# Weight loads in halves of 128 partitions, first loads in order of need, weight differences spread over tile 1

## The chip, the core and the metric

The kernel runs on one core of one Trainium2 chip. Times are microseconds (us) of that core. A time quoted for a kernel is the median of its runs, with the lowest and highest beside it. A profile shows one single execution. Its span is the time from the first to the last instruction, 1.7 us less than the time of the same execution (310.6 against 312.32 in the profile of the kernel before).

TensorE multiplies matrices, VectorE and ScalarE work on elements, GpSimd copies, casts and issues some transfers, and SyncE issues most transfers. In profile lines these are PE (PEld: its weight load), DVE, ACT, POOL and SP.

## The reference

Sliding-window attention (window 32), then a gelu feed-forward layer over all tokens:

```python
# q, k, v: (8, 8, 576, 64) fp32
scores = np.matmul(q, k.transpose(0, 1, 3, 2)) / np.sqrt(64)
mask = np.abs(pos[:, None] - pos[None, :]) <= 32
attn = softmax(np.where(mask, scores, -1e9))
x = np.matmul(attn, v).transpose(0, 2, 1, 3).reshape(4608, 512)
h = x @ w_in                    # w_in: (512, 2048)
out = gelu_tanh(h) @ w_out      # w_out: (2048, 512)
```

## The kernel before

The 4608 tokens go through the feed-forward layer in nine tiles of 512 (tile 0 to tile 8). A batch of attention (576 tokens) is done beside each tile. In a tile `ffn_in` multiplies by w_in and ScalarE takes the gelu; then `ffn_out` multiplies by w_out. Tile 0 uses 64 plain matmul positions; the other tiles use a Winograd form of seven products instead of eight (112 positions). That form needs four differences of w_out blocks, T1 to T4, computed once by VectorE.

What attention does between the matmuls is written in plans: at position i, do these acts. s is a score (matmuls and Exp), m a mask, v the weighing of V with its sum, x the final multiplication into xT. w and u cast a loaded w_out block, c is a weight difference, d pairs a chunk of V. g = -1 is the "tail", the group of the last queries of a batch; its Exp result is called `pet`.

```python
PLAN = {4: "s0@0 s1@1 v-1", 16: "m0 m1 x-1", 33: "s2@0 v0@1 v1", 36: "m2", 44: "x0", 50: "x1",
        62: "s3@0 s4@1 v2", ...}
PLAN_0 = {0: "s2@0 m0 m1 w1", 4: "s3@1", 12: "w2", 17: "c1", 18: "s-1@0 m2 m-1", 24: "m3",
          28: "v-1@1 x-1", 32: "d0 d1", 36: "d2 d3", 44: "v0@0 v1@1 x0 x1", 46: "w3",
          48: "v2@0 v3@1", 52: "u3", 54: "x2", 58: "x3", 60: "c2"}
PLAN_1 = PLAN | {0: "s-1@1 m-1", 4: "s0@0 v-1", 10: "s1@1"}
```

Loads: the first batch's q and k go over two queues, then V, then w_in in four blocks of two halves each. The third block (i == 2) is split by partitions, 120 and 8:

```python
    def load_w_in(i, w, c0=0, c1=4):
        for r in (slice(0, 120), slice(120, 128)) if i == 2 else (slice(0, 128),):
            nc.sync.dma_start(w[r, c0:c1, :], w_in_v[r, c0:c1, 512 * i:512 * i + 512])
        return w
    ...
    qk(0, nc.scalar)     # q on SyncE's queue, k on ScalarE's
    tails_0("k")
    qk(2, nc.scalar)
    qk(4, nc.scalar)
    qk(6)
    load_table(exp_set)
    vs()
    wi = []
    for i in range(4):
        wi.append(load_w_in(i, stage_w(), 0, 2))
        load_w_in(i, wi[i], 2, 4)
```

The prologue does batch 0's attention. `turn` transposes a pair of heads, `turned` does this with the next pair's casts, and `spin` is dummy matmuls that keep TensorE's clock up:

```python
    cast_early(0, 0, split)
    turn(0, 0)
    cast_tails(0, nc.vector, odd)
    cast_early(0, 1, split)
    trans_out(0, 0, pts[0], nc.scalar.copy)
    spin(1)
    trans_tails(0, psO.tile([128, 8, 128], FP16, name="pt", tag="O"), odd)
    spin(1)
    turned(1, 1, nc.scalar.copy)
    score(0, 0, 0)
    spin(1)
    turned(2, 0, nc.scalar.copy)
    score(0, 1, 1)
    ...
```

Casts, differences and weighing:

```python
    def cast_w(w, dst, on_dve=(0, 1), cs=range(4), on_act=()):
        for c in cs:
            (nc.scalar.copy if c in on_act else nc.vector.tensor_copy if c in on_dve else nc.gpsimd.tensor_copy)(
                dst[:, c, :], w[:, c, :])
    def combine(i, eng):                        # T1 .. T4
        dst, x, y = wino["todo"][i]
        eng.tensor_tensor(dst, x, y, op=ALU.subtract)
    ...
            for fc in range(begun, NF):
                ffn_in(t, fc)
                if t == 1 and fc in (8, 12):
                    combine(fc // 4 + 1, nc.vector)
    ...
                elif kind == "v":
                    bb, gg = group(g)
                    o, d = weigh(bb, gg, at)   # sums with ones, then times V
                    ods[g] = (o, invert(bb, gg, d))
```

## Time and profile before

| | before |
|---|---|
| median of the first 3 runs | 309.49 us (308.96 to 309.91) |
| the profiled execution | 312.32 us, span 310.6, mean granted clock 0.982 |
| TensorE enters the w_in matmuls of tile 0 | 21.55 us |
| tile 1 starts | 63.73 us |
| tile 2 starts | 100.89 us |

The second row became the main lesson: the profiled execution lies 2.83 us above the median. The page lines that carry the argument stand in the prediction. One line more, the shares of the chain that ended last, by engine:

```profile
PE 76%; DMA 12%; DVE 6%; SPq 3%; ACT 1%; issue 1%; DVEq 0%
```

The reader is to see that 12% of the span, some 37 us, is spent waiting for transfers. All of it lies in the first 48 us; from tile 2 on the tiles run with TensorE full.

### The profile page before, as it was taken

The page shows a single profiled execution, that of the slowest core. Times are in us where ns is not written, and L with a number is a line of the kernel's source. Part 1 is how long each engine was busy: PE and PEld are TensorE (multiplying, and loading weights), DVE is VectorE, ACT ScalarE, POOL GpSimd, SP SyncE. Part 2 cuts the span into 40 slices and gives each one's busy share as a digit, 9 for nine tenths or more (in the row PEclk, how much of TensorE's full clock was granted, in tenths as well). Part 3 has the DMA queues.
Part 4 walks back from the last instruction along what each step waited for, and adds up shares of the span by engine and source line. Part 5 has one row for each costly group of instructions (what it writes and reads, how often), then busy time and mean ns, then how long its engine had stood idle before and what let it go on. Part 6 is the DMA issues. An engine that isn't in the chain of part 4 may idle for free.

```text
span 310.6 us, 7121 instructions
## 1 busy us (share of the span) xinstructions
PE 291.3 (94%) x2896; PEld 183.4 (59%) x2896; DVE 199.1 (64%) x444; ACT 190.4 (61%) x296; POOL 92.3 (30%) x143
## 2 busy tenths in 40 slices
PE   6888887899699999999999999999999999999994
PEld 2543443444378458845874587468746864684583
DVE  3473478579676867686768577857785743632452
ACT  4595762666646577667766775787478757705600
POOL 4432548110640505150516053323350040006000
PEclk9799999999789999999999999999999999999999
DMA  7999999999796799998999799969896013004013
GB/s 218 249 321 291 315 333 244 229 256 210 166 212 90 141 149 237 149 149 141 243 155 186 95 241 170 177 142 215 110 135 149 2 39 98 3 0 136 2 34 101
DMA packets 116564, 50.73 MB, mean 163 GB/s; under 512 B 97925, under 2 KB 109957, under 8 KB 116532
## 3 DMA queue, kind: packets, MB, share of 16 engines
q1 hardware_dynamic: 87190, 37.73, 59.5%
q0 software_dynamic: 27776, 10.83, 24.4%
q10 hardware_dynamic: 1566, 1.74, 1.7%
q8 instruction: 22, 0.36, 0.5%
q14 instruction: 10, 0.08, 0.1%
HBM read 36.70 MB, written 9.44 MB: 149 GB/s over the span
## 4 chain that ended last, share of the span: by engine, by line
PE 76%; DMA 12%; DVE 6%; SPq 3%; ACT 1%; issue 1%; DVEq 0%
PE mm L594 32%; PE mm L496 18%; PE ph L496 15%; DMA wst<-in_moe_w_out_dram 4%; DMA wst<-in_moe_w_in_dram 4%; PE ps_s L388 3%; PE ps_d L411 2%; DVE s L539 2%; DMA qr<-in_q_dram 2%; PE ps_o L421 2%; DMA tr<-in_k_dram 2%; SPq L200 2%; SPq L143 2%; DVE t L529 1%; PE mm L568 1%; PE py L568 1%
## 5 line engine op out<-in xcount | busy, mean ns | idle before, releaser
L496 PEld LDWEIGHTS <-w_in 128*128 128x128 f16 x576 | 56.3, 98 | 68.3 <-issue 2.7
L496 PE MATMUL mm<-xT,w_in 128*128 128x512 f16 x320 | 78.2, 379 | 0.7 <-DVE yo L574 0.7
L504 ACT ACTIVATE gT<-mm 128x512 f16<-128x512 f32 x80 | 47.7, 597 | 43.4 <-PE mm L496 42.6
L496 PE MATMUL ph<-xT,w_in 128*128 128x512 f16 x256 | 64.5, 379 | 1.2 <-ACT gT L504 1.1
L558 POOL DMA_DIRECT2D out_dram<-y x55 | 33.1, 610 | 94.9 <-DVE y L623 85.8
L594 PEld LDWEIGHTS <-s 128*128 128x128 f16 x512 | 50.1, 99 | 6.4
L539 DVE TENSOR_TENSOR s<-gT 128x512 f16<-128x512 f16 x64 | 27.2, 426 | 35.0 <-ACT gT L504 35.0
L594 PE MATMUL mm<-t,s 128*128 128x256 f16 x376 | 45.6, 276 | 0.0
L504 ACT ACTIVATE gT<-ph 128x512 f16<-128x512 f32 x64 | 36.4, 600 | 12.5 <-PE ph L496 12.5
L400 ACT ACTIVATE pe<-ps_s 128x960 f16<-128x960 f32 (+1 forms) x32 | 30.6, 975 | 16.6 <-PE ps_s L388 16.4
L594 PEld LDWEIGHTS <-gT 128*128 128x128 f16 x384 | 36.3, 99 | 7.0
L594 PE MATMUL mm<-w_out,gT 128*128 128x256 f16 x256 | 34.3, 280 | 0.0
L447 ACT ACTIVATE lt<-lt 128x480 f32<-128x480 f32 (+3 forms) x40 | 23.5, 587 | 1.3
L92 ACT ACT_TABLE_LOAD x17 | 21.8, 1283 | 3.1 <-issue 2.4
L446 ACT ACTIVATE lt<-ps_d 128x480 f32<-128x480 f32 (+2 forms) x29 | 16.0, 552 | 10.5 <-PE ps_d L411 7.4
L406 DVE TENSOR_TENSOR pe<-pe,band 128x960 f16<-128x960 f16 x28 | 18.5, 680 | 1.7 <-ACT pe L400 1.7
L175 POOL DMA_DIRECT2D V<-in_v_dram x20 | 17.9, 909 | 1.2 <-issue 0.9
L421 PEld LDWEIGHTS <-V 128*64 128x64 f16 x520 | 14.7, 112 | 4.4 <-DVE V L190 0.8
L594 PE MATMUL mm<-t,gT 128*128 128x256 f16 x128 | 16.3, 273 | 0.0
L388 PE MATMUL ps_s<-QT,KT 64*64 64x128 f16 (+3 forms) x576 | 14.1, 221 | 0.7 <-DVE KT L312 0.7
L539 DVE TENSOR_TENSOR s<-s,gT 128x512 f16<-128x512 f16 x32 | 13.9, 434 | 1.1
L594 PE MATMUL mm<-w_out,s 128*128 128x256 f16 x120 | 14.4, 273 | 0.0
(103 smaller groups left out, 320.4 us busy)
## 6 DMA issues: line engine op xcount, KB each, us to landing
kr<-in_k_dram SPq DMA_DIRECT2D x29, 256.0 KB, 9.0
qr<-in_q_dram SPq DMA_DIRECT2D x6, 1024.0 KB
wst<-in_moe_w_in_dram SPq DMA_DIRECT2D x6, 512.0 KB, 9.0
wst<-in_moe_w_out_dram SPq DMA_DIRECT2D x3, 1024.0 KB
V<-in_v_dram POOLq DMA_DIRECT2D x20, 128.0 KB, 8.4
qr<-in_q_dram SPq DMA_DIRECT2D x8, 256.0 KB, 6.1
vr<-in_v_dram SPq DMA_DIRECT2D x8, 256.0 KB, 6.3
out_dram<-y POOLq DMA_DIRECT2D x6, 192.0 KB, 6.3
```

The source lines that it names most:

```text
L92: nc.scalar.add_instruction(mybir.InstLoadActFuncSet(name=nc.get_next_instruction_name(), act_func_set_id=which, ins=[], outs=[]))
L175: nc.gpsimd.dma_start(V[:, c, :, :], v[b, :, 128 * c:128 * c + 128, :].rearrange("h p d -> p h d"))
L388: nc.tensor.matmul(ps[64 * half:64 * half + 64, h, 4 * n * r:4 * n * r + 4 * n].rearrange("k (j p) -> k j p", j=4)[:, :, p0 - q0:p1 - q0], ...
L400: nc.scalar.activation(pe, ps[:, :, 0:w], AF.Exp, scale=SCALE)
L406: nc.vector.tensor_tensor(pe, pe, m.rearrange("k (o j) p -> k o j p", o=1).broadcast_to(list(pe.shape)), op=ALU.mult)
L421: nc.tensor.matmul(o[64 * h:64 * h + 64, cols].rearrange("d (j p) -> d j p", j=4)[:, :, p0 - q0:p1 - q0], Vs[b % 2][:, slot, 2 * pr + h, : ...
L447: nc.scalar.activation(lt[:, 0:n], lt[:, 0:n], AF.Exp, scale=-1.0)
L496: nc.tensor.matmul(ph, w_in16[:, dc, fc * 128:fc * 128 + 128], xT[:, dc, t * 512 % RING:t * 512 % RING + 512], start=(dc == 0), stop=(dc = ...
L504: nc.scalar.activation(gTs[t][:, fc, :], phs[fc], AF.Gelu_apprx_tanh)
L539: nc.vector.tensor_tensor(dst, x, y, op=op)
L558: eng.dma_start(out_v[b, j, q0 + p:q0 + p + e, cols], yo[m:m + e, cols])
L594: nc.tensor.matmul(pys["apart"][:, 0:256] if apart else py[:, blk, :], lhsT, wino[w][:, f, :], start=(new and i % (8 if one else 16) == 0) ...
```

## The change

The intent is to reach tile 2 sooner: load the third w_in block as fast as the others, score the first pair before the second is transposed, and keep weight differences away from the tail's mask. The core of the diff:

```diff
-PLAN_0 = {0: "s2@0 m0 m1 w1", 4: "s3@1", 12: "w2", 17: "c1", 18: "s-1@0 m2 m-1", 24: "m3",
-          28: "v-1@1 x-1", 32: "d0 d1", 36: "d2 d3", 44: "v0@0 v1@1 x0 x1", 46: "w3",
-          48: "v2@0 v3@1", 52: "u3", 54: "x2", 58: "x3", 60: "c2"}
-PLAN_1 = PLAN | {0: "s-1@1 m-1", 4: "s0@0 v-1", 10: "s1@1"}
+PLAN_0 = {0: "s2@0 m0 m1 w1", 4: "s3@1", 12: "w2", 18: "s-1@0 m-1 m2", 24: "m3", 30: "v-1@1 x-1",
+          32: "d0 d1", 36: "d2 d3", 44: "v0@0 v1@1 x0 x1", 46: "w3", 48: "v2@0 v3@1", 52: "u3", 54: "x2", 58: "x3",
+          60: "c1"}
+PLAN_1 = PLAN | {0: "s-1@1 m-1", 4: "s0@0", 10: "s1@1", 14: "v-1", 22: "c3", 56: "c4"}
...
 
-        def qk(h0, other=nc.sync):
-            for src, dst, queue in ((q, qr, nc.sync), (k, kr, other)):
+        def qk(h0, queues=(nc.sync, nc.sync)):
+            for src, dst, queue in zip((q, k), (qr, kr), queues):
                 queue.dma_start(
...
     def load_w_in(i, w, c0=0, c1=4):
-        for r in (slice(0, 120), slice(120, 128)) if i == 2 else (slice(0, 128),):
-            nc.sync.dma_start(w[r, c0:c1, :], w_in_v[r, c0:c1, 512 * i:512 * i + 512])
+        nc.sync.dma_start(w[:, c0:c1, :], w_in_v[:, c0:c1, 512 * i:512 * i + 512])
         return w
...
     qk, tails_0, vs = load_early(0)
-    qk(0, nc.scalar)
+    qk(0, (nc.sync, nc.scalar))
     tails_0("k")
-    qk(2, nc.scalar)
-    qk(4, nc.scalar)
+    qk(2, (nc.scalar, nc.sync))
+    qk(4)
     qk(6)
...
 
-    def turned(g, i, copy=nc.vector.tensor_copy):
-        turn(g, i)
-        if g < 3:
-            cast_early(0, g + 1, split)
-        trans_out(0, g, pts[g], copy)
-
     def pieces(tag, name):
...
     cast_tails(0, nc.vector, odd)
+    trans_out(0, 0, pts[0], nc.scalar.copy)
+    spin(2)
+    trans_tails(0, psO.tile([128, 8, 128], FP16, name="pt", tag="O"), odd)
     cast_early(0, 1, split)
-    trans_out(0, 0, pts[0], nc.scalar.copy)
     spin(1)
-    trans_tails(0, psO.tile([128, 8, 128], FP16, name="pt", tag="O"), odd)
+    score(0, 0, 0)
+    turn(1, 1)
+    cast_early(0, 2, split)
+    trans_out(0, 1, pts[1], nc.scalar.copy)
     spin(1)
-    turned(1, 1, nc.scalar.copy)
-    score(0, 0, 0)
-    spin(1)
-    turned(2, 0, nc.scalar.copy)
+    turn(2, 0)
+    cast_early(0, 3, split)
+    trans_out(0, 2, pts[2])
     score(0, 1, 1)
     cast_vt(0)
+    sums_of(0)
     spin(1)
-    sums_of(0)
     score(0, 2, 0)
+    turn(3, 1)
+    trans_out(0, 3, pts[3])
+    sums_of(1)
     spin(1)
-    turned(3, 1)
-    sums_of(1)
     score(0, 3, 1)
...
     os[0], os[1] = bank(0), bank(1)
-    s1 = psS.tile([128, 2, 512], FP32, name="ps_o", tag="S1")
-    os[2], os[3] = s1[:, 0, :], pieces("S0", "ps_o")
-    for g in range(2):
+    s0 = psS.tile([128, 2, 512], FP32, name="ps_o", tag="S0")
+    os[2], os[3] = s0[:, 0, :], pieces("S1", "ps_o")
+    for g in range(3):
         times(0, g, os[g], groups[(0, g)], (0, 1, 2, 4, 5))
-    spin(1)
+    spin(1, 512, s0[:, 1, :])
     sums_of(3)
-    for g in range(2, 4):
-        times(0, g, os[g], groups[(0, g)], (0, 1, 2, 4, 5))
-    spin(3, 512, s1[:, 1, :])
+    times(0, 3, os[3], groups[(0, 3)], (0, 1, 2, 4, 5))
+    spin(2, 512, s0[:, 1, :])
     cast_v(0, 3)
     for c in range(4):
-        cast_w(wi[0], w_in16[:, :, 0:512], (3,), (c,), (1,))
+        cast_w(wi[0], w_in16[:, :, 0:512], (3,), (c,))
     spin(3, 512, pieces("D", "spin"))
...
                 ffn_in(t, fc)
-                if t == 1 and fc in (8, 12):
-                    combine(fc // 4 + 1, nc.vector)
+                if t == 1 and fc == 8:
+                    combine(2, nc.vector)
                 if t == 1 and fc in (3, 4, 5, 6):
...
                     cs = (0, 1) if g == 3 else range(4)
-                    cast_w(wo[g], w_out16[:, 4 * g:4 * g + 4, :], cs=cs, on_act=(1,))
+                    cast_w(wo[g], w_out16[:, 4 * g:4 * g + 4, :], cs=cs, on_act=(1, 3))
                     if g == 2:
                 elif kind == "u":
-                    cast_w(wo[g], w_out16[:, 4 * g:4 * g + 4, :], on_dve=(2,), cs=(2, 3))
+                    cast_w(wo[g], w_out16[:, 4 * g:4 * g + 4, :], on_dve=(2,), cs=(2, 3), on_act=(3,))
                     cast_tails(1, nc.gpsimd)
```

The new plan puts T1 at the end of tile 0 ("c1" at 60), T2 in the w_in phase of tile 1, and T3 and T4 at positions 22 and 56 of tile 1.

> **What bounds the kernel now.** I read the busy shares first, then the chain of waits, then the timeline where that chain is not TensorE.
>
> ```profile
> PE 291.3 (94%) x2896; PEld 183.4 (59%) x2896; DVE 199.1 (64%) x444; ACT 190.4 (61%) x296; POOL 92.3 (30%) x143
> ...
> PEclk9799999999789999999999999999999999999999
> DMA  7999999999796799998999799969896013004013
> ```
>
> TensorE is busy 94% of 310.6 us, so over most of the run only fewer matmuls would help, and the diff removes none. But PEclk has a dip in slices 11 and 12 (78 to 93 us), and DMA is full for the first 47 us. From 101 us on, the tiles run with TensorE busy 30.50 of 30.50 us (the windows view of 101 to 131.5): what is won before 101 us reaches the end unchanged. The chain of waits, early part:
>
> ```profile
> 17.10 11.50 DMA wst<-in_moe_w_in_dram
> 28.62 5.74 DMA qr<-in_q_dram
> 34.35 12.90 DMA wst<-in_moe_w_out_dram
> ...
> 47.61 1.63 DVE t L529
> 49.24 0.98 DVE pe L406
> 50.23 0.76 DVE pet L406
> ```
>
> From 17 to 47 us loads set the pace; then the weight difference T1 (L529) and two masks stand on the path. The windows view compares stretches of equal kind (columns: length, busy time of five engines, granted clock, DMA share, GB/s):
>
> ```profile
> 21.00:27.30 6.30, 5.11 (x24) 2.14 (x23) 3.92 (x9) 4.25 (x7) 1.49 (x2) 1.00 1.06 227
> 28.00:34.00 6.00, 6.00 (x29) 2.74 (x28) 2.12 (x9) 4.18 (x7) 3.53 (x6) 1.00 1.07 352
> 38.00:44.00 6.00, 4.36 (x91) 2.73 (x91) 5.95 (x12) 4.25 (x5) 2.18 (x4) 1.00 1.05 382
> ...
> 78.00:82.20 4.20, 1.10 (x37) 0.77 (x29) 4.11 (x7) 3.51 (x4) 2.52 (x3) 0.88 0.70 102
> 81.20:88.00 6.80, 5.80 (x47) 3.95 (x47) 3.37 (x8) 2.33 (x4) 5.27 (x8) 0.50 0.86 230
> ```
>
> Two things stand out. In 21 to 27.3 us the DMA is busy but moves 227 GB/s, against 382 for the same 2048-byte rows of w_out. That is when the third w_in block passes, the one loaded as 120 and 8 partitions: by its packets, one takes 140 to 190 ns there and 84 to 88 ns before and after. And in tile 1 TensorE works 1.10 of 4.20 us, then 6.8 us at half clock. The timeline there:
>
> ```profile
> 78.17 1.62 DVE L529 TENSOR_TENSOR t<-w_out,t 128x2048 f16<-128x2048 f16 x1
> 81.59 0.55 DVE L406 TENSOR_TENSOR pet<-pet,band 128x768 f16<-128x768 f16 x1
> 82.20 0.53 PE L411 MATMUL ps_d<-pet,ones 128*64 128x384 f16 x2 [3.10 <-DVE pet L406]
> 51.02 0.30 PE L411 MATMUL ps_od<-pet,ones 128*64 128x256 f16 x2 [1.77 <-DVE pet L406]
> ```
>
> Twice the tail group's mask (pet) comes late because VectorE computes a weight difference first; TensorE stands 3.10 us in tile 1 and 1.77 us in tile 0.
>
> **What the Trainium skill says.** DMA: Bandwidth & Descriptors, section "Why a DMA increments its semaphore by 16 and not by 1": a DMA is split over the largest number of engines up to 16 that divides its outer dimension, so 120 partitions take 15 engines and 8 take 8. The trace agrees: the 120-partition DMA shows one of its 16 completion marks at 16.84 us, straight after issue, and 15 from 22.78 us on. Its section "The descriptor swizzle" says that in a 128-partition load each engine writes one SBUF port; a 15-engine split need not, which would explain the doubled packet time; no run yet shows the cause. TensorE: Matmul & The Clock Gate, Part 1: about 3.4 us of idleness drops the clock to half, in free-running windows. The trace agrees: the idle stretch 79.0 to 82.2 us, then clock 0.50 for 6.83 us (two periods of 3.41). DMA page, "Issuing engines are not separate DMA queues": which engine issues a load changes no bandwidth; so the new queue assignment of the first loads can only reorder.
>
> **The change, part by part.**
>
> 1. *Halves of 128 partitions.* The slow stretch moved some 1.43 MB (227 GB/s by 6.3 us); at the 385 GB/s seen on either side this takes 3.7 us, a gain of 2.6 us. By engine: a normal engine needs 16 packets x 84 ns = 1.34 us per half block; the slowest engine landed the second block at 24.32, the third at 28.60, the fourth at 31.09 us. From 21.50 us (first half of the second block) five halves at 1.34 us end at 28.2 us, so 2.9 to 3.2 us earlier. Also two fewer DMAs share the eight completion lanes that SyncE rotates through. Everything queued behind shifts by about 3 us: q and k of batch 1, w_out, and later k of batch 2, whose last chunk landed at 68.72 us and released the VectorE casts at 68.80 us.
>
> 2. *First loads in order of need, first pair scored earlier.* The k tails landed at 7.00 us behind two k pairs on the other queue; I estimate 6.4. Score 0 no longer waits for the second pair's transposes (10.29 us): KL copied by about 7.8 us, so its Exp starts near 8.7 instead of 11.41. But ScalarE is busy 9.20 of 10.20 us between 10.4 and 20.6, and V chunk 3 (15.80 us) and w_in's first halves (18.52 and 19.83 us) land no earlier. My pass through the queues (Exp 1.0, Ln+Exp 1.22, QT copy 0.6, spread 0.65 us each) puts the last spread at 21.35 instead of 23.06 us; TensorE enters w_in about 2 us earlier. This is then overtaken by part 1 and is not added.
>
> 3. *Tile 0.* T1 leaves position 17 (1.63 us), m-1 goes ahead of m2 (about 1 us), the third chunk of each w_out block moves from GpSimd to ScalarE. The w_out 2 block lands at 47.25 - 3.2 = 44.0; ScalarE then casts two chunks (1.25), does the pet Exp (0.6), VectorE masks (0.75): v-1 runs at 46.6 instead of 51.02, a gain of 4.4, of which 1.2 is beyond the DMA shift. Position 44 follows at 50.5 (12 + 2 matmuls x 0.216, plus v-1 itself), where V chunk 3 of batch 1 (52.36 - 3.2, cast, pairing) is also just ready; was 54.94. Tile 1 starts at about 59.3 instead of 63.73.
>
> 4. *Tile 1.* VectorE's chain starts with the k casts at 65.5 (DMA shift only). From 68.80 to 82.14 it took 13.3 us, including both differences; one (1.62) leaves, and the wait for the last gelu is gone: pet is masked at about 77.0. v-1 now stands at position 14, behind 14 matmuls and score 1, so TensorE idles about 1.1 us for pet's Exp (score 1 needs its bank) instead of 3.1, and the half clock should not come. Position 16 is reached at 77.9 instead of 86.17.
> Not all of this stays. After pet, VectorE pairs V of batch 2, whose last GpSimd cast (ended 82.62) moves only to 78.3; then it owes M1 copy 0.65, masks 1.2, x-1 0.55, T3 1.22, U2 0.69, m2 0.65, pairing 0.84 twice, x0 0.7, C11 0.67, x1 0.7: that is 87.0, and v2 at position 62 waits for x1. So position 62 runs at 87.7 instead of 94.68: **7.0 us** gained. T4 (1.22) fits before position 80.
>
> Sum: part 1 gives 3.2, the pet waits and half clock a further 3.8 after VectorE takes some back. 309.49 - 7.0 = 302.5; I give 0.4 back for lags such as contended differences (1.62 instead of 1.22). **302.9 us.**
>
> **The rivals.**
> - *VectorE becomes the bound in tile 1.* T3 and T4 now fall where TensorE works (VectorE busy 9.11 of 13.00 us between 88 and 101); if they collide with evictions more than reckoned, 1.5 us more is lost: 304.5. For it: the list above is already VectorE end to end.
> - *The slow stretch is not the partition split* but HBM or the column block. Then part 1 is nothing, tile 0 gains 1 to 2, tile 1 about 3.5: 304.5 to 305.5. Against it: blocks 1, 2 and 4 read the same layout at full speed.
> - *Loads stay on the path through one lagging engine.* An instruction fetch of 16 KB takes 1.2 to 1.3 us of one engine (16, 28, 45, 61 us) and the last of 16 marks counts. Then the shift is 2 instead of 3 us: about 304.
> - *The half clock trips anyway*: 3.4 us back, 306.
> - *The early loads alone matter not at all*, since later loads bound the end: already assumed.
>
> **Range and chances.** The rivals cost 1 to 3.4 us each and rarely come together; gains beyond the sum would need the V casts of batch 2 to come earlier too, up to 2 us. Eight in ten: 300.6 to 305.8. The 2% line is 303.3, just above the estimate: faster 0.56, same 0.43, slower 0.01.
>
> **What would show it.** Right: 2048-byte packets near 84 ns and over 350 GB/s through the third block; its last landing near 25, w_out 2's near 44 us; T1 absent before v-1 in tile 0; tile 1 starting at 59 to 60; no half clock near 80 us; the w_in phase of tile 2 starting near 94 us instead of 101. Wrong: GB/s still near 230 in 21 to 25 us; VectorE waiting for k of batch 2 beyond 67 us; TensorE waiting on x1 or U2 for over 1.5 us in tile 1; clock 0.50 again.

## The result, and the profile after

| | before | after |
|---|---|---|
| median, same chip | 309.68 us (308.96 to 309.91, 4 runs) | 304.91 us (304.43 to 305.74, 4 runs) |
| ratio of fast runs | 1 | 0.9853 (0.9825 to 0.9880) |
| the profiled execution | 312.32 us, clock 0.982 | 304.9 us, clock 0.992 |

A ratio is the mean time of one kernel's fast runs over the mean of the other's fast runs of the same rounds, so not quite the ratio of the medians quoted. The kernel after is about 1.5% faster: inside the predicted range, but on the slower side, and not past the 2% that I had held likeliest. The gain is 4.8 us of medians, where I had reckoned 6.6.

The page of the kernel after, busy shares, granted clock by slices and the chain by engine:

```profile
PE 288.1 (95%) x2896; PEld 181.6 (60%) x2896; DVE 197.1 (65%) x445; ACT 190.6 (63%) x297; POOL 89.0 (29%) x141
...
PEclk9799999999999999999999999999999999999999
...
PE 83%; DVE 6%; DMA 4%; ACT 3%; issue 1%; SPq 1%; POOL 0%
```

The reader is to see three things against the lines of before. TensorE is busy 3.2 us less in all (291.3 to 288.1) with the same 2896 matmuls. The dip to 7 and 8 in slices 11 and 12 of PEclk is gone. And transfers carry 4% of the chain instead of 12%.

The timeline of the kernel after, at the places of the prediction (start, duration, engine, line, operation, output and inputs, and in brackets the idle time before it and what ended it):

```profile
25.99 1.89 PE L495 MATMUL ph<-xT,w_in 128*128 128x512 f16 x8 [1.13 <-ACT gT L503]
...
46.02 0.74 DVE L405 TENSOR_TENSOR pet<-pet,band 128x512 f16<-128x512 f16 x1 [1.24 <-ACT pet L399]
47.68 0.30 PE L410 MATMUL ps_od<-pet,ones 128*64 128x256 f16 x2
60.14 1.21 DVE L528 TENSOR_TENSOR t<-w_out 128x2048 f16<-128x2048 f16 x1
...
77.26 0.56 DVE L405 TENSOR_TENSOR pet<-pet,band 128x768 f16<-128x768 f16 x1 [0.27 <-ACT pet L399]
77.28 0.40 PE L387 MATMUL ps_s<-QT,KT 64*64 64x96 f16 x16 [0.88 <-ACT pet L399]
...
86.92 0.42 PE L420 MATMUL ps_o<-pe,V 128*64 128x96 f16 x14 [0.49 <-DVE xT L455]
```

In tile 0 the mask now waits for the Exp on ScalarE (1.24 us of VectorE idle), not for T1, and v-1 at 47.68 follows with no wait shown on TensorE. T1 runs at 60.14, at the end of tile 0. In tile 1 TensorE's largest wait is 0.88 us, for pet's Exp, where it was 3.10 us for pet's mask in the first profile of before. v2 waits 0.49 us for x1, as the prediction had said it would.

The chain of waits of the kernel after, in tile 1 (start, duration, what):

```profile
71.16 6.30 DMA qr<-in_v_dram
77.51 0.80 POOL V L283
78.33 0.42 DVE V L182
...
81.57 0.72 DVE t L528
```

Here is what now sets the middle of tile 1: V of batch 2 lands at 77.46 us, is cast on GpSimd and paired on VectorE, and VectorE's list from there (M1, the masks, T3 and x1) releases v2 at 86.92 us. In the kernel before, no transfer stood on the chain after 47.25 us.

The same places in the windows view (length, busy time of PE, PEld, DVE, ACT and POOL, granted clock, DMA share, GB/s):

```profile
21.00:25.30 4.30, 3.86 (x18) 1.67 (x17) 2.74 (x7) 2.44 (x5) 1.48 (x2) 1.00 1.05 390
...
74.00:78.20 4.20, 3.33 (x67) 2.04 (x66) 2.38 (x5) 3.90 (x6) 1.70 (x3) 1.00 0.99 118
78.20:83.00 4.80, 4.80 (x86) 3.94 (x86) 4.66 (x8) 3.38 (x6) 3.68 (x6) 1.00 1.03 283
```

The third w_in block passes at 390 GB/s instead of 227, and tile 1 runs at clock 1.00 where it ran at 0.50.

| milestone, us in the profile | before | predicted | after |
|---|---|---|---|
| third w_in block landed | 28.60 | near 25 | 25.29 |
| w_out 2 landed | 47.25 | 44.0 | 44.34 |
| TensorE enters w_in | 21.55 | 2 earlier | 20.38 |
| v-1 of tile 0 | 51.02 | 46.6 | 47.68 |
| tile 1 starts | 63.73 | 59.3 | 60.27 |
| pet masked in tile 1 | 81.59 | 77.0 | 77.26 |
| position 62 of tile 1 (v2) | 94.68 | 87.7 | 86.92 |
| tile 2 starts | 100.89 | near 94 | 93.48 |

By these two profiles the prediction was right: 7.4 us gained by tile 2, where it had said 7.0. By the clock on the wall the gain was 4.8. From the start of tile 2 both profiles take 209.7 us to their end (310.6 - 100.89 and 303.2 - 93.48), so nothing was given back later. Something was in the profile of before that is not in most of its executions.

### The profile page after: what moved, and what is told of

The parts are those of the page before. It is cut to its first block, busy times and chain, and to the rows that moved or that the text cites. A ratio compares the mean times of both kernels' runs of the same rounds, so it can differ in the third digit from the quotient of the medians.

```text
span 303.2 us, 7115 instructions
## 1 busy us (share of the span) xinstructions
PE 288.1 (95%) x2896; PEld 181.6 (60%) x2896; DVE 197.1 (65%) x445; ACT 190.6 (63%) x297; POOL 89.0 (29%) x141
## 4 chain that ended last, share of the span: by engine, by line
PE 83%; DVE 6%; DMA 4%; ACT 3%; issue 1%; SPq 1%; POOL 0%
PE mm L593 30%; PE mm L495 21%; PE ph L495 17%; PE ps_s L387 3%; PE ps_d L410 2%; DMA qr<-in_v_dram 2%; PE ps_o L420 2%; PE mm L567 2%; DMA tr<-in_k_dram 2%; PE py L567 1%; ACT gT L503 1%; DVE xT L455 1%; ACT lt L445 1%; PE ps_od L410 1%; SPq L347 1%
## 5 line engine op out<-in xcount | busy, mean ns | idle before, releaser
L495 PE MATMUL ph<-xT,w_in 128*128 128x512 f16 x256 | 64.5, 379 | 1.2 <-ACT gT L503 1.1
L593 PE MATMUL mm<-t,s 128*128 128x256 f16 x376 | 44.7, 273 | 0.0
L593 PE MATMUL mm<-w_out,gT 128*128 128x256 f16 x256 | 33.2, 273 | 0.0
L446 ACT ACTIVATE lt<-lt 128x480 f32<-128x480 f32 (+3 forms) x40 | 23.5, 587 | 1.3
```

Of the source, the lines that this page charges most:

```text
L446: nc.scalar.activation(lt[:, 0:n], lt[:, 0:n], AF.Exp, scale=-1.0)
L495: nc.tensor.matmul(ph, w_in16[:, dc, fc * 128:fc * 128 + 128], xT[:, dc, t * 512 % RING:t * 512 % RING + 512], start=(dc == 0), stop=(dc = ...
L593: nc.tensor.matmul(pys["apart"][:, 0:256] if apart else py[:, blk, :], lhsT, wino[w][:, f, :], start=(new and i % (8 if one else 16) == 0) ...
```

## The experiments

Three questions stood at first. Is it the split of partitions that slows the packets of all transfers in flight, and is it worth most of the gain? Is the half clock in tile 1 worth about 3 us in every run, or does it come in only some executions? And is the early scoring hidden behind the loads, or does it matter, through the clock or through the order? Where a text on record uses a letter, P is the theory of partitions and ports, and C that of the clock. Twelve runs were made, in three groups, each group on its own chip with its own runs of before (medians 310.37, 309.58 and 310.48 us). Ratios are to those, of fast runs alone. Half clock means that the records show a granted clock of 0.50.

### The kernel before once more, and with its idle stretch filled

The first is the kernel before, unchanged. The second does twelve dummy matmuls while TensorE waits for pet in tile 1:

```diff
                     bb, gg = group(g)
+                    if t == 1 and g < 0:
+                        spin(12, 512, pieces("D", "spin"))
                     o, d = weigh(bb, gg, at)
```

> The kernel before, unchanged. Theory A (the half clock in tile 1 belongs to some executions only): most executions show a mean granted clock of 0.99 or more and a span near 307.8 us; those with 0.98 are 2.5 to 3 us longer, like the profiled one (310.6 us, clock 0.982). Theory B (the timed executions all have the half clock and the profiled one was slow for another reason): clock 0.98 in all, spans spread without regard to the clock.

> The kernel before with 12 dummy matmuls (2.6 us) in the hole of TensorE in tile 1, ahead of the sums of the tail group. The hole itself stays, only the clock cannot drop. Theory A: no half clock near 81 us in the profile, span near 307.5 us, and the median of the timed runs moves less than 1 us, since most of them had no drop. Theory B: the median falls by about 3 us, to 306.5.

Measured: the unchanged kernel 311.83 us (309.21 to 314.84, 6 runs, the highest in the slow state), ratio 1.0026 (0.9972 to 1.0081); the filled one 310.42 us (309.81 to 311.59), ratio 1.0003 (0.9962 to 1.0045). The filled kernel, timeline and windows:

```profile
79.67 2.76 PE L231 MATMUL spin<-KT 128*128 128x512 f16 x12
82.48 0.35 PE L411 MATMUL ps_d<-pet,ones 128*64 128x384 f16 x2
```

```profile
77.50:82.00 4.50, 4.50 (x52) 2.19 (x51) 4.32 (x7) 3.97 (x5) 2.58 (x3) 1.00 0.96 128
82.00:88.00 6.00, 5.94 (x106) 4.47 (x105) 3.82 (x8) 3.05 (x6) 4.94 (x7) 1.00 1.14 268
```

The dummies fill the hole and the clock stays at 1.00 through 82 to 88 us, where before had 0.50. Tile 2 starts at 98.52 instead of 100.89. Yet the time does not move: 1.0003. The profile of the unchanged kernel says why. It has the hole and no half clock in tile 1. Tile 1 as a whole, first of the first profile of before, then of this second one (timeline line, then windows line):

```profile
63.73:100.89 37.16, 34.06 (x351) 21.89 (x351) 27.83 (x60) 23.74 (x35) 10.46 (x15) 0.91 1.08 193
```

```profile
84.16 0.35 PE L411 MATMUL ps_d<-pet,ones 128*64 128x384 f16 x2 [2.23 <-DVE pet L406]
```

```profile
66.56:100.19 33.63, 31.40 (x350) 20.52 (x350) 27.68 (x60) 23.74 (x35) 9.94 (x15) 1.00 1.14 198
```

The same program takes 37.16 us for tile 1 in one execution and 33.63 in the other. The second is 31.40 us of work and one wait of 2.23. So the half clock in tile 1 is not worth its 3 us in every run. Neither theory of the first expectation came as stated. Theory A wanted clocks of 0.99 or more in most executions; of the 17 of this group two have that, and they took 311.78 and 313.45 us. Ten lie at 0.986 to 0.988. A mean clock tells how many periods of half clock an execution had, but not where: the profiles with 0.985 to 0.987 show two of them (beside the end of the run), at 8 us (before again), at 10 and 44 us (filled), or at 9 and 81 us (the split of 112 and 16 below), the first profile with 0.982 three. So more than half of the executions of before (21 of the 39 in all groups have 0.984 to 0.988) seem to have two periods, and in only some of them one of the two lies in tile 1.

Why one and not the other? The records of the clock change only at multiples of 3.41 us, and so I took TensorE's busy share in each such stretch (a window), for 14 profiles. Of the windows at full clock, the last 10 us of the runs left out, every one with a share of 0.51 or less was followed by a window at half clock; none with 0.62 or more was; those between went either way. (In the last 10 us one with 0.50 was not followed by half clock. A window that is itself at half clock can be followed by another with more: 0.70 at 81.18 us in the first profile.) In the first profile of before, the hole fell into one window (77.76 to 81.18 us, share 0.39). In the second it lay across two (0.60 and 0.75). So it fits that a hole of 2 to 3 us is caught or not by where the windows happen to lie.

### The w_in halves alone, and the change without them

The first is the kernel before with only the load changed; the second is the kernel after with only the load put back:

```diff
-        for r in (slice(0, 120), slice(120, 128)) if i == 2 else (slice(0, 128),):
-            nc.sync.dma_start(w[r, c0:c1, :], w_in_v[r, c0:c1, 512 * i:512 * i + 512])
+        nc.sync.dma_start(w[:, c0:c1, :], w_in_v[:, c0:c1, 512 * i:512 * i + 512])
```

> The kernel before with the third block of w_in in halves of 128 partitions, nothing else. Theory (a 120-partition load slows every packet that is in flight with it): packets of the third block take 84 to 90 ns, the block's last landing comes near 25.5 us instead of 28.6, the last chunk of w_out block 2 near 44.3 instead of 47.25, and about 3 us of it reach the end: 306.5 us. Rival (the column block or HBM is slow there): still about 227 GB/s and 140 to 190 ns per packet between 21 and 27 us, time unchanged at 309.5. Second rival (loads are hidden once the masks wait for T1): the loads land 3 us earlier but the time falls by less than 1 us.

> The changed kernel with the third block of w_in again as 120 and 8 partitions. If the partition split carries most of the gain: 308 to 309 us, with packets of 140 to 190 ns back between 21 and 27 us. If the new plans carry it: 306 us or less.

Measured: alone 309.06 us (306.75 to 310.41), ratio 0.9940 (0.9892 to 0.9987); the change without it 308.34 us (307.43 to 313.88, the highest in the slow state), ratio 0.9920 (0.9872 to 0.9968). The windows view, first of the halves alone, then of the kernel after with 120 and 8:

```profile
21.00:27.00 6.00, 5.04 (x23) 2.11 (x22) 4.22 (x10) 4.11 (x7) 2.40 (x4) 1.00 1.05 385
```

```profile
21.00:27.00 6.00, 3.96 (x18) 1.48 (x16) 1.70 (x6) 2.66 (x5) 1.74 (x2) 1.00 1.07 230
```

The split decides the rate, with all else equal: 385 against 230 GB/s, and by the trace's transfer records (medians of each microsecond from 21 to 26 us) 84 to 88 ns against 139 to 181 ns a packet of 2048 bytes. The third block landed at 25.34 us in the first. That the split is the cause is shown. Its worth is smaller than the shift: 0.6%, some 1.9 us, although the loads come 3 us earlier; the 306.5 us that the theory expected were missed. In tile 1 TensorE still waits for pet's mask; the waits view (what waits, for what, total us, number, longest):

```profile
PE ps_d L410 <- DVE pet L405: 2.6, 1, 2.6
```

### Another split: 112 and 16

By the rule quoted in the prediction, 120 partitions go to 15 engines and 8 to 8; 112 and 16 both divide by 16. If a missing engine were the cause, this would be fast.

```diff
-        for r in (slice(0, 120), slice(120, 128)) if i == 2 else (slice(0, 128),):
+        for r in (slice(0, 112), slice(112, 128)) if i == 2 else (slice(0, 128),):
```

> The kernel before with the third block of w_in split as 112 and 16 partitions. Both parts divide by 16, so by the skill's page all 16 engines take part in each. Theory P (not the missing engine but the spread of an engine's rows over SBUF ports slows the packets): the packets are slow again, 130 ns or more and under 260 GB/s between 21 and 27 us. Theory E (the load that leaves out an engine is at fault): 84 to 95 ns and over 350 GB/s, block landed near 25.5 us.

One look: 309.32 us. The windows view:

```profile
21.00:25.00 4.00, 3.94 (x20) 1.67 (x18) 3.14 (x7) 2.11 (x3) 1.49 (x2) 1.00 1.07 241
```

It is as slow, 241 GB/s, 132 to 152 ns a packet (medians as above, 21 to 25 us), and the third block landed at 27.19 us. So by that rule it isn't the number of engines. What is left is which partitions each engine writes (by the same rule a 112-partition load gives each engine 7 partitions, not 8), or that a second, small load runs beside the large one: both slow splits have it, and no run separates the two. That several engines then write through one port would explain it; the trace has no record of ports, so this stays argued. By the way, this profile has one window of half clock in tile 1 (80.73 to 84.14 us, after a window of share 0.35), where the first profile of before had two.

### The plans alone, and the change with the old plans

The first puts only the plans, the places of T1 to T4 and the `on_act` of the casts into the kernel before; the second puts the old ones back into the kernel after:

```diff
-PLAN_1 = PLAN | {0: "s-1@1 m-1", 4: "s0@0 v-1", 10: "s1@1"}
+PLAN_1 = PLAN | {0: "s-1@1 m-1", 4: "s0@0", 10: "s1@1", 14: "v-1", 22: "c3", 56: "c4"}
   (and PLAN_0, combine and on_act as in the change)
```

> The kernel before with the new plans alone: weight differences T1 to T4 at their new places, m-1 ahead of m2, v-1 of tile 1 at position 14, a third w_out chunk per block on ScalarE. Theory (the masks come before the differences, but w_out block 2 still lands near 47.3 us and k of batch 2 near 68.7 us): v-1 of tile 0 near 50 us instead of 51, TensorE's wait for pet in tile 1 gone (under 1.2 us in all), no half clock near 81 us; 308 to 309 us, ratio 0.993 to 0.998. Rival (VectorE takes it all back with T3 and T4 among the evictions): ratio 1.00.

> The changed kernel with the old plans put back: halves of 128 and the new prologue alone. The halves alone gave 0.994. Theory (the two parts need each other: earlier loads are worth less while T1 and T4 sit ahead of the masks): ratio 0.990 to 0.994, with a wait for pet of over 2 us in tile 1. Rival (the parts simply add): ratio 0.988 or less.

Measured: alone 308.79 us (307.41 to 309.58), ratio 0.9975 (0.9927 to 1.0022); the change with the old plans 307.50 us (306.31 to 308.85), ratio 0.9939 (0.9889 to 0.9989). The timeline of the latter, then of the plans alone:

```profile
48.78 0.30 PE L410 MATMUL ps_od<-pet,ones 128*64 128x256 f16 x2 [1.56 <-DVE pet L405]
...
78.24 0.56 DVE L405 TENSOR_TENSOR pet<-pet,band 128x768 f16<-128x768 f16 x1 [0.25 <-ACT pet L399]
78.85 0.35 PE L410 MATMUL ps_d<-pet,ones 128*64 128x384 f16 x2 [2.23 <-DVE pet L405]
```

```profile
81.52 0.40 PE L388 MATMUL ps_s<-QT,KT 64*64 64x96 f16 x16 [0.88 <-ACT pet L400]
```

With the old plans both waits for pet are back, 1.56 and 2.23 us; with the new plans and the old loads 0.88 us for pet's Exp is left. So it is shown that the plans remove these waits.

What in them does it is not the same in both tiles. In tile 0 it is the order on VectorE, T1's place among it: the first profile of before has T1, then a mask, then pet's mask (the chain in the prediction). In tile 1 it is hardly the place of T4. In the line at 78.24 above, with the old plans, VectorE itself stood idle for 0.25 us until ScalarE had finished pet's Exp (78.21 us), and T4 was over at 75.83. In six of the seven profiles with the old plans pet's mask begins within 0.1 us of the end of pet's Exp; only in the first profile of before did it begin 0.9 us later (80.68 and 81.59 us). What is left is that v-1 went from position 4 to position 14: TensorE now has matmuls to do until the Exp is over. No run moved v-1 and T4 separately, so this reading stays argued. Nor is all of it won: TensorE's waits after the start of tile 1, up to the start of tile 2, add up to 2.2 to 2.6 us with the old plans, where tile 1 has no half clock and no dummies, and to 1.1 to 2.5 us with the new ones (0.47 of the 2.5, in the second profile of the kernel after, for pet's mask). The plans with the old loads are worth nothing that the runs can tell from zero.

### The early scoring alone, the change without it, and that with its hole filled

The prologue alone takes the load order and the prologue of the change into the kernel before. The second is the kernel after with both put back (as in the diff above, lines from `qk` to `cast_w(wi[0], ...)`). The third is the second with dummies around the tails' transposes:

```diff
-    spin(1)
+    spin(3)
     trans_tails(0, psO.tile([128, 8, 128], FP16, name="pt", tag="O"), odd)
-    spin(1)
+    spin(4, 512, pieces("D", "spin"))
     turned(1, 1, nc.scalar.copy)
```

> The kernel before with the new first loads and the new order of the first pairs alone. Theory (T1 and the 120-row load keep the path, as the loads did in the prediction): ratio 0.998 to 1.002, though TensorE enters w_in 1 to 2 us earlier. Rival (the old prologue costs a second half-clock window after 12 us, and the new one does not): ratio 0.993 to 0.997, clocks of 0.99 and more.

> The changed kernel with the old prologue: first loads and first pair as before. Theory (the prologue is overtaken by the loads and adds nothing or up to 1 us, since with the halves of 128 TensorE and not the loads bounds the w_in phase of tile 0): ratio 0.986 to 0.989; TensorE enters w_in near 21.5 us instead of 20.4. Rival (the prologue carries over 1.5 us): ratio 0.990 or more.

> The changed kernel with the old prologue, and five more dummy matmuls around the first tails' transposes, where TensorE stood still. Without them the ratio was 0.9936, against 0.985 for the changed kernel. Theory C (half of what the new prologue brings is clock: it keeps TensorE busy before 9 us, so that no second half-clock window follows): first w_in matmul near 21.5 us instead of 23.5, ratio 0.988 to 0.991, clocks of 0.99 and more. Rival O (the order of loads and scores alone): ratio stays at 0.992 to 0.995.

Measured: alone 310.39 us (309.02 to 311.88), ratio 1.0002 (0.9959 to 1.0045). The change without it 307.75 us (306.64 to 308.54), ratio 0.9936 (0.9884 to 0.9988): my theory had the early scoring as nearly worthless and expected 0.986 to 0.989, which was missed. With the dummies 307.49 us (306.14 to 308.88), ratio 0.9908 (0.9864 to 0.9951).

The change without its prologue, windows and timeline:

```profile
5.20:8.60 3.40, 1.08 (x12) 0.55 (x10) 0.42 (x1) 0.69 (x2) 0.74 (x2) 1.00 1.06 317
8.60:15.40 6.80, 4.93 (x63) 3.23 (x62) 3.52 (x7) 2.24 (x4) 3.20 (x5) 0.50 1.03 200
```

```profile
10.46 0.58 PE L230 MATMUL spin<-KT 128*128 128x512 f16 x1 [2.63 <-DVE KL L295]
```

And the kernel after in about the same stretch:

```profile
4.90:8.30 3.40, 1.71 (x19) 0.72 (x17) 1.66 (x5) 0.59 (x1) 0.92 (x2) 1.00 1.12 300
8.30:11.70 3.40, 3.40 (x44) 2.55 (x43) 1.15 (x4) 1.53 (x2) 1.68 (x3) 0.50 1.28 247
```

In the old order TensorE stands 2.63 us for the copied tails and the clock is halved for two windows; in the new order it is halved for one. The table below lets the two be told apart, in single profiles: with the old order TensorE enters w_in at 21.5 to 22.0 us where one window before that is at half clock (five profiles) and at 23.5 to 23.7 where two are (two profiles); with the new order at 20.38 with one and at 19.6 to 20.0 with none. So at one window each the order is worth some 1.2 to 1.6 us, and a second window costs some 1.5 to 2.2. The dummies' 0.9908 lies between: 0.3% back, with intervals that overlap. Their half clock was not gone, but came later, at 19.1 us, and the entry was at 22.50 instead of the 21.5 expected. So the ratios do not tell clock from order.

Why does the prologue give nothing alone and seem to give 0.6 to 0.8% on top of the rest? (The intervals of 0.9936 without it and 0.9876 with it overlap.) The starts in the profiles tell it; the last column is where the records show half clock, a period of 3.4 us each, without the end of the run:

| kernel | loads | plans | prologue | enters w_in | tile 1 starts | from one to the other | tile 1 | from tile 2 to the end | half clock at |
|---|---|---|---|---|---|---|---|---|---|
| before | old | old | old | 21.55 | 63.73 | 42.18 | 37.16 | 209.7 | 9; 81 twice |
| before, again | old | old | old | 23.71 | 66.56 | 42.85 | 33.63 | 209.6 | 8 twice |
| before, filled | old | old | old | 21.99 | 64.36 | 42.37 | 34.16 | 210.2 | 10; 44 |
| before, 112 and 16 | slow | old | old | 21.54 | 62.76 | 41.22 | 35.14 | 209.7 | 9; 81 |
| prologue alone | old | old | new | 19.56 | 63.53 | 43.97 | 33.67 | 210.1 | 43 |
| plans alone | old | new | old | 22.00 | 64.52 | 42.52 | 32.83 | 209.6 | 9; 44 |
| change, 120 and 8 | old | new | new | 19.60 | 62.92 | 43.32 | 33.62 | 210.4 | none |
| halves alone | new | old | old | 21.62 | 61.38 | 39.76 | 33.98 | 209.7 | 10 |
| change, old plans | new | old | new | 20.00 | 61.26 | 41.26 | 33.62 | 209.7 | none |
| change, old prologue | new | new | old | 23.52 | 63.15 | 39.63 | 33.91 | 209.7 | 9 twice |
| the same, filled | new | new | old | 22.50 | 61.94 | 39.44 | 33.78 | 210.2 | 19 |
| after | new | new | new | 20.38 | 60.27 | 39.89 | 33.21 | 209.7 | 8 |
| after, again | new | new | new | 19.71 | 59.81 | 40.10 | 34.65 | 209.7 | none |

With the slow loads, tile 1 starts at 62.8 to 64.5 us in six of seven profiles, whether TensorE enters w_in at 19.6 or at 22.0: an earlier entry becomes a longer wait. The three without half clock between entry and tile 1 say it best: entry at 19.60, 21.54 and 21.55, tile 1 at 62.92, 62.76 and 63.73. (Three others have a period of half clock at 43 or 44 us, behind a window of share 0.55 to 0.61 with waits of about 1 us for casts of w_out; no profile with the fast loads has one there. The seventh, with two periods early and an entry at 23.71, starts at 66.56.) With the fast loads tile 1 starts 39.4 to 40.1 us after the entry, wherever that lies between 19.7 and 23.5, in five of six profiles, the halves alone with the old plans among them: the core's own work sets the pace, and each microsecond of entry counts. The sixth, old plans with an early entry, takes 41.26, and there v-1 of tile 0 waits 1.56 us for pet's mask; in the halves alone, with the later entry, it did not wait. So each part uncovers the next limit: the loads, then the entry, then T1 ahead of the mask, and only the three together reach 60 us. By the ratios the sum of the parts alone is 0.8% (0.6, 0.25 and 0) and together they gave 1.2 to 1.5%, but the intervals are too wide to show a difference; the argument rests on the table.

The column of tile 1 tells the rest. Without half clock in it, it takes 33.6 to 34.2 us with the old plans and 32.8 to 34.7 with the new ones: no gain that a single profile could show.

### The kernel after once more, and a further version

The first is the kernel after, unchanged. The further version removes the wait of 1.13 us at 25.99 (columns 4 and 5 of the first tile share one PSUM tile, and the first matmul of column 5 waits for the gelu of column 4) and moves T3 ahead and the first pairing of V back:

```diff
-                if n == 4:
-                    phs["S"] = psS.tile([128, 2, 512], FP32, name="ph2", tag="S0")
-                phs[fc] = phs["S"][:, n % 2, :]
+                phs[fc] = psS.tile([128, 2, 512], FP32, name="ph2", tag=f"S{n % 2}")[:, 0, :]
...
-PLAN_1 = PLAN | {0: "s-1@1 m-1", 4: "s0@0", 10: "s1@1", 14: "v-1", 22: "c3", 56: "c4"}
+PLAN_1 = PLAN | {0: "s-1@1 m-1", 4: "s0@0", 14: "s1@1 v-1", 56: "c4"}
...
-                if t == 1 and fc == 8:
-                    combine(2, nc.vector)
+                if t == 1 and fc in (8, 12):
+                    combine(fc // 4, nc.vector)
...
-            if t == 1 and i in (0, 40):
-                pair_v(2, nc.vector.tensor_copy, slice(i // 10, i // 10 + 4))
+            if t == 1 and i in (18, 40):
+                pair_v(2, nc.vector.tensor_copy, slice(0, 4) if i == 18 else slice(4, 8))
```

> The changed kernel once more, beside the other three: the ratio on this chip, and the clock of each execution. Theory (its profiled execution was typical, that of the kernel before was not): median 304.5 to 305.5 us, ratio 0.983 to 0.988, most clocks 0.99 or more, while those of the kernel before lie at 0.98 to 0.987.

> The changed kernel with four moves that its profile suggests: the columns 4 and 5 of tile 0's w_in phase in separate PSUM tiles (TensorE waited 1.13 us for the gelu of column 4 before it wrote column 5), T3 in the w_in phase of tile 1 where VectorE waited 1.42 us, score 1 of tile 1 at position 14 instead of 10, the first half of batch 2's V pairing at position 18 instead of 0. Expected: 0.5 to 1.5 us below the changed kernel, 303.5 to 304.5 us. Rival (loads bound again): no change.

Measured: after again 306.11 us (305.14 to 308.56), ratio 0.9876 (0.9827 to 0.9926): the ratio as expected, the median 0.6 us above the expected range; five of six clocks are 0.99 or more, but so are three of the eleven of before. The further version 305.34 us (304.81 to 305.85 in five fast runs; a sixth was slow, 310.45 at clock 0.983), ratio 0.9836 (0.9796 to 0.9877). The expected 303.5 to 304.5 us were missed. The mean of its fast runs is 1.15 us below that of after in the same rounds, with intervals that overlap: it is faster than before, and whether it is faster than after the runs do not settle. Its timeline, then two lines of its waits:

```profile
23.25 2.75 PE L493 MATMUL ph<-xT,w_in 128*128 128x512 f16 x12
```

```profile
PE mm L565 <- POOL w_out L208: 1.4, 2, 1.1
...
PE ps_od L420 <- DVE V L183: 1.0, 1, 1.0
```

The wait of 1.13 us is gone; 1.4 us come back in tile 0 as a wait for GpSimd's casts of w_out, and 1.0 us for the pairing of V. The w_in phase ends 1.9 us earlier than in the kernel after (34.23 against 36.09 us), and tile 1 starts at 60.11 against 60.27 us (tile 2 at 94.00 against 93.48). GpSimd had itself waited 1.83 us for the load before the first of these casts. So in this profile the loads of w_out are the next limit of tile 0, as the loads of w_in were in the kernel before.

## Why the prediction was right or wrong

- **The transfers**: right. Predicted 385 GB/s for the third block and its landing near 25 us; measured 390 and 25.29. Undoing it alone brought 230 GB/s back. That the new queues of the first loads only reorder them was not tested apart from the rest.
- **Tile 0**: right in kind, somewhat too large. v-1 came 3.3 us earlier instead of 4.4. The w_out 2 block landed 0.3 us later than reckoned, and pet's mask was done at 46.76; v-1 came 0.9 us after that with no wait, so TensorE's own queue held it. I had not followed TensorE's work up to that point. Tile 1 started at 60.27 instead of 59.3.
- **The early loads and scoring**: here a step failed in reasoning: "This is then overtaken by part 1 and is not added." It is the other way round. Part 1 takes away the limit behind which the earlier entry was hidden, so the entry counts from then on: 1.9 to 2.6 us by the ratios (0.9936 without it against 0.9876 and 0.9853 with it, on three chips, the first two with overlapping intervals), a part of that being clock. The table shows it: 39.4 to 40.1 us from entry to tile 1. Since the profile of before had tile 1 start at 63.73 and I had set 59.3 through loads and masks, this error did not make the total wrong.
- **Tile 1**: the mis-sized term is "the pet waits and half clock a further 3.8 after VectorE takes some back". By the profile it was too small, if anything: tile 1 went from 37.16 to 33.21 us, 3.95. But 3.5 of this is the half clock of one execution (37.16 against 33.63 in the second profile of the same kernel). Against an execution without it the new plans gain 0.4 us in one profile and lose 1.0 in the other. Two readings behind this term were off. "Because VectorE computes a weight difference first" holds for 0.9 of the 3.10 us; for the rest the mask waited for pet's Exp, as it did wholly in other executions. And "the idle stretch 79.0 to 82.2 us, then clock 0.50" is out of order: TensorE went idle at 79.1 us, and the clock fell at 81.18, after 2.1 us of it; what went with the half clock was the busy share of the window, 0.39, and not the length of the hole.
- **The subtraction**: "309.49 - 7.0 = 302.5" takes a gain that was read from one execution of 312.32 us from a median of 309.49. From the execution that I had read, 312.32 - 7.0 = 305.3, against 304.91 measured. Or by the typical case, as an estimate from the table: tile 1 starts 3.5 us earlier (63.73 to 60.27), its length gains 0.4, and the half clock, in two of six profiles with the old plan in tile 1 (37.16 and 35.14 against 33.6), is worth (3.5 + 1.5) / 6 = 0.8 us on average. That is 4.7 us, and 309.68 - 4.7 = 305.0.
- **The rivals**: the half clock did not come back in tile 1, VectorE carried the chain of tile 1 from 78.3 to 86.9 us, as reckoned, but cost TensorE no more than 0.49 us for x1, and the slow stretch was the split. None of the rivals was what took the gain. The chances put faster by over 2% first, and that rested on the subtraction. That the median came to lie inside the range owes much to the width of the range, 5.2 us; the estimate was 2.0 us too low.

Open are three things: whether shared ports are why 120 or 112 partitions are slow, how much of the prologue's worth in the timed runs is clock, and what else makes executions of before differ. The 39 of the three groups spread from 308.1 to 314.8 us, four of them in the slow state. Of the 35 fast ones those with a mean clock of 0.982 or less average 311.5 us, those at 0.984 to 0.988 average 309.5, but the five at 0.989 and more average 311.0. So the clock is not the whole of it.

## What to carry to other kernels

Before subtracting a gain read in a profile, compare the time of the profiled execution with the median, and take the gain from the execution in which it was read; a stretch at half clock is a thing to look for in a second profile of the same kernel. When several limits lie within a microsecond or two of each other, parts of a change need not be worth their sum: measure each alone and each undone, and look at where the stage starts and how long it lasts. Before blaming what ran ahead of a late instruction, look at what that instruction itself waited for: in tile 1 pet's mask had T4 ahead of it, and in most executions waited for the Exp. A load like the ones here is better split by columns than by partitions: 120 or 112 of 128 partitions moved at 227 to 241 GB/s, all 128 at 385 to 390.

## What the Trainium skill lacked or had wrong

- DMA: Bandwidth & Descriptors, section "Why a DMA increments its semaphore by 16 and not by 1", gives the number of engines of a load, by which 112 partitions have 16 as 128 do; it says nothing of the rate. Here 112 and 16 moved 241 GB/s and 120 and 8 moved 227 to 230, against 385 to 390 for 128, and the packets of 2048 bytes took 132 to 181 ns (medians) instead of 84 to 88. No page says that such a split slows a load this much.
- DMA: Bandwidth & Descriptors, section "Latency and other measured facts", has its best guess for the engines that it calls usually slower in rings that only GpSimd's transfers use. Here, in the kernel after, the last of the 16 marks came 1.1 to 1.5 us behind the other 15 in seven loads in a row (17.2 to 25.3 us), after a packet of 16 KB of instructions had passed (14.81 to 16.12 us) and long before GpSimd issued its first transfer (60.4 us). In the kernel before, the first half of w_in had 15 of its marks by 17.46 us and the last at 18.52. After the packet at 43.9 us it was only 0.1 us, and the trace does not say which engine a packet or a mark belongs to, so the instruction fetch as the cause is argued.
- TensorE: Matmul & The Clock Gate, Part 1, speaks of idle windows, of gaps over some 3.4 us and, without a figure, of many short idle times. Here a window only half busy was enough: at full clock, and but for the end of the runs, each with a busy share of 0.51 or less was followed by half clock, none with 0.62 or more. The page says that the windows run freely, and so the start-up differs from run to run; what it lacks is that a hole of 2 to 3 us can thereby halve the clock in some executions and not in others of the same kernel, here 37.16 against 33.63 us for one tile.
